# Transposing and pooling as one product, one engine to a bank's eviction, an early activation table, and a new order of the steps

## The chip, the cores and the metric

The kernel runs on one core of a Trainium2 chip. The core has five engines with queues of their own: TensorE (PE; its weight loads are shown as PEld), VectorE (DVE), ScalarE (ACT), GpSimd (POOL) and SyncE (SP), which issues most of the transfers. Each takes its instructions in the order in which they were written and waits at semaphores. The metric is the device time of one execution in microseconds, the median over several runs. 1.2 and 2.4 GHz are the two levels of TensorE's clock; the profile gives the granted clock as a share of the upper one.

## The reference

Two parts follow each other. First attention over `q`, `k`, `v` of shape (2, 8, 576, 64), batch, heads, tokens and channels, as the sum of two kinds:

```python
q_d, k_d, v_d = means of q, k, v over groups of 4 tokens      # 144 groups
out_d   = softmax(q_d k_d^T / 8) v_d                          # pooled attention
out_up  = repeat(out_d, 4, axis=2)
mask    = abs(pos[:, None] - pos[None, :]) < 4                # a band of 7 tokens
out_loc = softmax(where(mask, q k^T / 8, -1e9)) v             # local attention
x = (out_up + out_loc).transpose(0, 2, 1, 3).reshape(1152, 512)
```

Then a mixture of four experts over all 1152 tokens, each with weights 512 x 1024 and 1024 x 512:

```python
p = domain_probs / (domain_probs.sum(-1, keepdims=True) + 1e-9)
out = sum over e of p[:, e:e+1] * (maximum(x @ w1[e], 0) @ w2[e])
```

All inputs and the output are 32-bit floats.

## The kernel before

**Attention.** There are four attention blocks, a0 to a3: two batches, and of each the two halves of 288 tokens. A half is three tiles (t = 0, 1, 2) of 96 tokens. A tile of `q` or `k` is loaded with tokens on the partitions, 96 x 512, and has to stand with channels on the partitions. The step `k00t.0` (batch 0, half 0, tile 0) or `a0.qt.0` does this on TensorE: four transposes of 96 columns into one PSUM bank (line 391). For batch 0's keys and for a0's queries, nine tiles in all, four more products with a 96 x 24 pooling matrix (line 397) put the sums over four tokens beside them in the same bank. Two eviction steps follow, `k00te.0` for the tokens and `k00tp.0` for the sums; the table `ENGINE` gives each of them to ScalarE (A), VectorE (V) or GpSimd (G). The banks of these steps come from a pool of three (`ps_g`), so that a fourth tile waits for the first one's eviction.

Local scores are the steps `a0.sc0.0` and so on: 64 small products per tile (line 561) with, in a0 alone, a product of the identity with the mask ahead of them (line 551). `max`, `sub`, `exp`, `sum`, `rec`, `norm` are the softmax, `blk` transposes of 32 x 32 on VectorE, and `pv` the product with `v`. The pooled attention has the steps `ds` (scores, line 721), `dm`, `de`, `da`, `db`, `dq` (softmax), `dt` (transposes), `dc`, `dv` and `xd`. `v01s` and `v00s` are the pooled `v` of batch 0 (line 479). `xs`, `xh` and `xl` add both kinds up and split the result into a high and a low part; every large product is taken as three products of such parts.

**Experts.** Expert 0 runs in four chunks of tokens, m00 to m03: `m` is the first product (line 828), `r` and `l` evict it, `o` is the second (line 853). Chunk m00 needs only a0's result, m01 also a1's, m02 part of a2's, and m03 all of a3's, so the chunks lie between the steps of attention. The weights are loaded raw (`raw100`), and split by `whi` and `wlo`. Experts 1 to 3 follow (the late experts, lines 1084 and 1273), from the step `p110` on.

**The order.** Every step is a small function with a name. The list `ORDER` names all of them, and each engine's queue is its steps in that order; nothing is scheduled at run time. `WARM` gives the products of zeros that the steps `warm0` to `warm4` run on TensorE, in units of half a 512-column product. The helpers' lines 178, 180, 184 and 186 record most evictions of both engines. SP's loads stand in the same list, and a load whose target is still being read waits on SP with all loads behind it.

Of the kernel before, what the change touches and what calls it, by code (L numbers as in the profile page):

```python
# [21 lines left out]
ORDER = """
    k01r.0 a0q.2 pool warm0 k01t.0 a0.qt.2 k00r.1 k00t.1 k01r.1 kstart0 k00tp.1 k01r.2 k01tp.0 a0.start k01te.0 warm1
    k01t.1 k00te.1 k01te.1 a0q.0 k01tp.1 a0.qtp.2 a0.qte.2 k01t.2 a0.qt.0 a0q.1 k00r.0 mask a0.qt.1 a0.qtp.1 k01te.2
    a0.qte.0 a0.qtp.0 clear0 k00r.2 k01tp.2 v01n.1 clear1 k00t.0 a0.qte.1 vw00e vw00 k00t.2 k00tp.2 k00tp.0 warm2
    a0.ds0 k00te.2 k00te.0 a0.sc0.0 a0.dm0 a0.de0 a0.ds1 a0.dm1 a1q.2 a0.sc0.1 a0.de1 a0.max0 a0.da0 warm3 a0.ds2
    a0.db0 a0.dq0 a0.sub0 a0.da1 a0.db1 a0.sc1.0 a0.dt0 a0.sc1.1 a0.exp0 a0.sum0 a0.dc0 a0.dm2 a0.ds3 a0.dm3 v01n.0
    a0.sc2.0 a0.max1 a0.dq1 a0.dt1 a0.dc1 a1q.0 a0.de2 a0.da2 a0.sc2.1 a1.qt.2 a0.max2 a0.de3 a0.sub2 a0.exp2 poolw
    a1.start a1.qte.2 a0.sub1 a0.da3 a0.exp1 a0.rec0 a0.sum2 a0.rec2 a0.norm0 a1.qt.0 a0.db2 a0.norm2 a0.blk0.1
    a1.qte.0 v01n.2 v01s v01de vw01 a0.dq2 a1q.1 a0.db3 a0.sum1 a1.qt.1 a1.qte.1 a0.rec1 a0.blk0.0 vw02 v00s a0.norm1  # L30
    a0.blk1.0 v00de a1.sc1.1 a1.sc1.0 a1.qd.1 a0.dq3 a0.dt3 a0.dc3 a0.dv0 a0.dv1 raw100 a0.pv0 whi100.0 wlo100.0
    whi100.1 wlo100.1 a1.qd.0 a0.blk1.1 a0.blk2.1 a0.dt2 a0.dc2 a0.blk2.0 a0.dv2 a1.sc2.1 a0.dv3 a2q.0 a0.xd a0.xs0
    a0.xh0 warm4 a1.ds0 a1.ds1 a1.dm1 a0.pv1 a1.dm0 a1.de1 a1.de0 a1.sc0.1 a0.xs1 a0.xh1 a0.xl1 a1.da1 a1.db1 a0.pv2
    a1.sc2.0 a0.xs2 k10r.1 a0.xh2 a0.xl2 a1.sc0.0 a2q.2 a1.ds2 a1.ds3 k11r.2 a1.dq1 a1.madd0 a0.xl0 raw101 whi101.1
    kstart1 a1.max0 a1.dt1 vw03 m00.m0 a1.dc1 k10r.2 a1.da0 wlo101.1 m00.r0 a1.db0 m00.m1 m00.m2 k10t.2 a1.madd1
    a1.dq0 whi101.0 a2.start a1.sub0 a1.dt0 raw200 a1.dm2 a1.max1 a1.dm3 a1.de2 wlo101.0 m00.m4 m00.l0 m00.r1 a1.madd2
    a1.max2 a1.sub2 m00.l1 m00.r2 a1.dc0 k10r.0 k10t.0 a1.de3 whi200.1 a1.exp0 a1.sum0 k10t.1 a1.da2 wlo200.1 a1.da3
    a1.sub1 k10te.2 k10te.0 a2q.1 a2.qt.1 a2.qte.1 m00.l2 whi200.0 wlo200.0 m00.m7 a1.rec0 praw k11r.1 k10te.1 k10d.0
    a1.db3 a1.dq3 k11t.1 k11r.0 k11te.1 k11t.0 k11te.0 raw201 a1.norm0 a1.blk0.0 a2.qt.2 m00.r7 a1.exp2 a1.sum2 m00.m3
    m00.r3 m00.l7 a1.exp1 a1.dv0 a1.blk0.1 m00.r4 a1.sum1 vw04 a1.db2 a2.qt.0 a1.rec1 m00.l4 v10n.0 a2.qte.0 k11t.2  # L40
    a2.qte.2 a1.dq2 m00.m5 a1.rec2 k11te.2 a1.dv1 vw05e a1.norm2 a1.dt3 whi201.0 a2.qd.0 k11d.1 a1.dt2 m00.r5 a1.norm1
    m00.l5 m00.o10 a1.dc2 a2.qd.1 a1.dv2 a1.pv0 a1.blk2.1 m00.l3 v10n.1 a1.dc3 a1.dv3 a1.xd a1.xs0 v10d.0 a1.blk2.0
    a2.sc1.1 m00.o00 m00.m6 m00.r6 a3q.0 k11d.0 a2.ds0 a3q.1 a1.blk1.1 a2.dm0 a2.sc2.0 wlo201.0 a1.blk1.0 a2.sc2.1
    a2.sc0.0 a2.sc0.1 a2.madd0 vw10e a2.de0 a2.da0 a2.db0 a2.sc1.0 a2.madd1 vw05 a1.pv2 a1.xh0 a2.max0 a2.sub0
    a3.start a1.pv1 a1.xs2 a1.xh2 vw11 m00.l6 a1.xs1 m00.o01 a2.madd2 a2.max1 a2.sub1 whi201.1 a2.ds1 a2.dm1 a2.de1
    a2.dq0 a1.xl0 wlo201.1 a2.da1 a2.exp0 a2.sum0 a3q.2 m00.o11 m00.o12 a2.db1 m00.o13 a2.exp1 a1.xh1 m00.o02 m00.o03
    a2.max2 a2.sub2 v11n.1 a2.exp2 a3.qt.1 a2.sum2 a2.rec2 a2.dt0 v10d.1 a3.qt.2 a1.xl2 a3.qte.2 a1.xl1 m01.m6 gate
    a3.qte.1 k10d.1 a2.ds2 m01.r6 v11n.0 v11d.0 m00.g0 m01.l6 a2.rec0 a2.ds3 a2.dm3 a2.de3 a2.da3 a2.db3 m01.m3 m01.r3
    vw14 a2.sum1 m01.l3 a2.rec1 m01.m7 a2.dc0 m01.m1 m01.r1 v11d.1 a3.qt.0 a3.qte.0 a2.norm0 a2.dq1 a2.dt1 m00.g1
    a2.norm1 a2.blk1.1 a2.norm2 a2.dc1 a3.sc1.0 a2.blk1.0 a3.sc1.1 m01.l1 m01.r7 m01.l7 a3.sc2.1 a3.sc2.0 vw10 a2.dv0  # L50
    a2.dm2 a2.de2 a2.dv1 a2.blk0.1 a2.dq3 a2.dt3 a2.dc3 m01.m0 m01.r0 m01.m2 a2.blk0.0 a2.pv0 a2.da2 a2.db2 a2.dq2
    a3.qd.0 m01.r2 a3.madd2 a2.dt2 a2.dc2 a2.dv2 a2.dv3 vw15e a2.xd a2.xs0 a2.xh0 a2.blk2.1 m01.m5 a3.ds0 a2.blk2.0
    a2.pv1 m01.r5 m01.l2 a3.dm0 a3.de0 a3.sc0.0 a3.sc0.1 a3.madd0 m01.l0 m01.m4 a3.max0 m01.r4 m01.o00 m01.o01
    a3.madd1 m01.l5 a2.xs1 m01.l4 m01.o02 m01.o03 a3.qd.1 a3.max2 a3.sub2 a3.ds1 a3.dm1 a3.de1 a3.max1 a2.xh1 a2.xl0
    a3.sub1 m01.o10 a3.sub0 m01.o11 m01.o12 a3.da1 a3.db1 a2.xl1 vw12 a3.ds2 a3.dm2 a3.exp2 a3.exp1 a3.dq1 a3.sum1
    a3.dt1 m01.g0 a3.rec1 a3.de2 a3.da2 a3.db2 a3.dq2 a3.sum2 m01.o13 m02.m5 m02.r5 m02.l5 a3.dc1 a3.da0 a3.db0 m02.m4
    a3.exp0 a3.sum0 a3.dv1 a3.dt2 a3.dc2 a2.pv2 m01.g1 a3.rec0 m02.m3 m02.m1 a2.xs2 m02.r4 m02.l4 m02.r3 m02.l3
    a3.norm0 vw13 a3.blk0.0 a3.ds3 a3.dm3 a3.de3 a3.rec2 m02.r1 m02.m0 m02.r0 m02.m6 m02.m2 m02.r2 m02.r6 a3.dv2
    m02.l1 a3.blk0.1 a3.da3 a3.db3 a3.dq3 a3.dt3 a3.dc3 m02.l0 a2.xh2 a2.xl2 a3.norm2 a3.dq0 a3.pv0 m02.l2 a3.blk2.1
    a3.norm1 a3.blk1.0 a3.blk1.1 a3.dt0 a3.dc0 a3.dv0 a3.blk2.0 vw15 a3.dv3 a3.xd m02.m7 m02.r7 m02.o10 m02.l6 a3.xs0  # L60
    m02.o11 a3.xh0 a3.xl0 m02.o12 a3.pv2 a3.xs2 a3.pv1 m02.o00 m02.o01 m02.o02 a3.xs1 a3.xh2 m02.l7 m02.o13 a3.xh1
# [1372 lines left out]
```

## Time and profile before

| what | us |
|---|---|
| median of 3 runs | 461.78 (461.69 to 464.54) |
| the profiled execution | 460.38 |
| its span, first to last instruction | 458.5 |
| TensorE busy in the span | 444.9 |
| VectorE busy | 321.2 |
| ScalarE busy | 196.4 |
| GpSimd busy | 102.3 |

The busy time of an engine is the union of its instructions' times. A busy TensorE may still run at the lower clock, so its share is read beside the granted clock. The chain of waits follows the work that ended last back to the start: a piece of it is either work on an engine or time to issue.

### The profile page before, as it was taken

To read this page: it belongs to the slowest core of one execution; us is meant where nothing else is said; L and a number is where in the kernel's file an instruction comes from. 1 tells how busy PE (TensorE), PEld (TensorE's weight loads), DVE (VectorE), ACT (ScalarE), POOL (GpSimd) and SP (SyncE) were. 2 spreads that over 40 slices of the span, in tenths; PEclk is the share of its full clock that TensorE was granted. 3 is DMA by queue.
4 is the path that set the end of the run, shared out by engine and by line. 5 is a ranking of instruction groups with operands and counts; after the bars stand their busy time and mean duration, and the time that the engine had idled before them with its cause. 6 is when DMAs were issued, how large, how long until landed. Compare 5 with 4: busy or idle time off the path is not lost.

```text
span 458.5 us, 10026 instructions
## 1 busy us (share of the span) xinstructions
PE 444.9 (97%) x4181; PEld 420.4 (92%) x4181; DVE 321.2 (70%) x569; ACT 196.4 (43%) x389; POOL 102.3 (22%) x142
## 2 busy tenths in 40 slices
...
PEclk8578999999999999999999999999999999999999
...
GB/s 171 116 183 113 181 226 42 121 4 24 4 44 46 2 1 43 183 143 76 76 126 93 70 207 93 47 75 91 112 93 114 164 91 48 46 52 91 44 92 162
DMA packets 75494, 42.52 MB, mean 93 GB/s; under 512 B 36920, under 2 KB 73400, under 8 KB 75448
## 3 DMA queue, kind: packets, MB, share of 16 engines
...
q14 instruction: 13, 0.11, 0.1%
...
## 4 chain that ended last, share of the span: by engine, by line
PE 95%; DVE 2%; ACT 1%; issue 1%; POOL 1%; DVEq 0%; ACTq 0%
PE ps L1084 29%; PE ps L1273 26%; PE ps L1286 4%; PE m03h L828 4%; PE m03o L853 4%; PE m01h L828 3%; PE m02h L828 3%; PE m00h L828 3%; PE m00o L853 2%; PE m02o L853 2%; PE m01o L853 2%; PE vs L479 1%; PE a_qt L391 1%; PE wps L274 1%; PE k00t L397 1%; PE k01t L397 1%
## 5 line engine op out<-in xcount | busy, mean ns | idle before, releaser
L1273 PE MATMUL ps<-slot,unit 128*128 128x256 f32 x1008 | 119.9, 280 | 1.1 <-DVE unit L1193 1.1
L1273 PEld LDWEIGHTS ps<-slot,unit 128*128 128x128 f32 x1008 | 119.0, 189 | 1.3 <-DVE unit L1193 1.3
L1084 PE MATMUL ps<-xhi,slot 128*128 128x288 f32 x384 | 66.4, 294 | 0.0
L1084 PE MATMUL ps<-xc,slot 128*128 128x288 f32 x432 | 60.4, 295 | 0.0
L1084 PEld LDWEIGHTS ps<-xc,slot 128*128 128x128 f32 x432 | 58.3, 188 | 0.1
L1084 PEld LDWEIGHTS ps<-xhi,slot 128*128 128x128 f32 x384 | 56.3, 188 | 0.1
L1133 POOL DMA_DIRECT2D raw<-in_moe_w_dram x15 | 19.5, 1297 | 143.1 <-DVE slot L1139 82.6
L1096 ACT ACTIVATE H<-ps 128x288 f32<-128x288 f32 x72 | 27.6, 412 | 50.8 <-PE ps L1084 50.8
L184 ACT CAST slot<-raw 128x1024 fp32r<-128x1024 f32 (+1 forms) x33 | 41.7, 1280 | 9.1 <-DVE raw L1032 9.1
L1100 DVE TENSOR_TENSOR H<-H,ps 128x288 f32<-128x288 f32 x72 | 29.7, 449 | 20.6 <-PE ps L1084 20.5
L1038 DVE TENSOR_TENSOR slot<-raw,slot 128x1792 fp32r<-128x1792 f32 x12 | 24.3, 2022 | 25.3 <-PE ps L1084 21.1
L1084 PE MATMUL ps<-xlo,slot 128*128 128x288 f32 x192 | 41.1, 295 | 0.0
L1188 ACT ACTIVATE unit<-H 128x1024 fp32r<-128x1024 f32 x18 | 19.1, 1062 | 28.9 <-PE ps L1273 17.4
L1084 PEld LDWEIGHTS ps<-xlo,slot 128*128 128x128 f32 x192 | 30.7, 188 | 0.0
L1171 DVE SCALAR_TENSOR_TENSOR H<-H 128x1024 f32<-128x1024 f32 (+1 forms) x18 | 28.1, 1575 | 3.5 <-ACT H L1098 3.2
L1184 ACT ACTIVATE unit<-H 128x512 fp32r<-128x512 f32 (+1 forms) x24 | 20.0, 844 | 23.2 <-DVE H L1100 13.6
L1139 DVE TENSOR_TENSOR slot<-raw,slot 128x1024 fp32r<-128x1024 f32 x21 | 25.3, 1218 | 2.4 <-ACT slot L184 2.4
L1197 DVE SCALAR_TENSOR_TENSOR unit<-H,unit 128x1024 fp32r<-128x1024 f32 x18 | 22.0, 1222 | 7.1 <-ACT unit L1188 7.0
L1193 DVE SCALAR_TENSOR_TENSOR unit<-H,unit 128x512 fp32r<-128x512 f32 (+1 forms) x24 | 22.5, 952 | 1.5 <-ACT unit L1184 1.5
L1295 DVE SCALAR_TENSOR_TENSOR acc<-ps,npr,acc 128x256 f32<-128x256 f32 x48 | 20.7, 477 | 3.1 <-PE ps L1273 2.9
L636 DVE STREAM_TRANSPOSE ptb<-pmb 32x256 f32<-32x256 f32 x48 | 20.9, 435 | 2.1 <-PE a0pv L645 0.7
...
## 6 DMA issues: line engine op xcount, KB each, us to landing
...
```

The lines of the kernel that those rows point to most:

```text
L184: nc.scalar.copy(out_, in_)
L828: nc.tensor.matmul(ps[:, :n], w[:, d, cc:cc + P], x[:, d, n0:n0 + n], start=i == 0, stop=i == len(terms) - 1,)
L853: nc.tensor.matmul(ps[:, cs], T[f"{nm}t{f}"][:, hpart, cc:cc + P], w[:, f % 4, cs], start=f == 0 and x == 0, stop=f == KF - 1 and x == 2,)
L1038: engine(f"wo{e}{i}").tensor_tensor(w1tile(i, 1), raw1(e, i), f32(w1tile(i, 0)), ALU.subtract)
L1084: nc.tensor.matmul(bank(acc_, n, i)[:, :NH // 2], w[:, d * P:(d + 1) * P], x[:, d, n * (NH // 2):(n + 1) * (NH // 2)], start=u == 0 and fi ...
L1096: nc.scalar.mul(dst, at, -1.0)
L1100: nc.vector.tensor_tensor(dst, dst, at, ALU.add)
L1139: engine(f"bo{e}{m}").tensor_tensor(w2tile(m, 1), raw2(q), f32(w2tile(m, 0)), ALU.subtract)
L1171: nc.vector.scalar_tensor_tensor(at[o], at[x], 0.0, at[y], ALU.max, op)
L1193: nc.vector.scalar_tensor_tensor(o, x, 0.0, y, ALU.max, ALU.subtract)
L1197: nc.vector.scalar_tensor_tensor(o, x, -1.0, y, ALU.mult, ALU.subtract)
L1273: nc.tensor.matmul(ps[:, t * 256:t * 256 + 256], a[:, f, t * P:t * P + P], b[:, f], start=first_ and (t, f, x) == (0, 0, 0), stop=(t, f, x ...
```

## The change

- The tile `ident` becomes `idt`, whose first 24 columns are a pooling matrix and whose next 128 are the identity. For the nine tiles that are pooled on TensorE, one ordinary product of 120 columns takes the place of a transpose of 96 and a product of 24. The other fifteen tiles keep their transposes.
- One step evicts both parts of a bank, on one engine; the steps `tp` are gone.
- The pooling matrices are made by a memset and two selections instead of copies and additions. The values that `v01s` needs get a step of their own, `poolm`.
- A copy of one column on ScalarE at the very start brings the activation table load there.
- `WARM` goes from 16, 2, 2, 4, 2 to 24, 2, 2, 2; `ENGINE` and `ORDER` are new for everything up to `endfirst`; from `p110` on the order is as before.

```diff
-WARM = [16, 2, 2, 4, 2]
+WARM = [24, 2, 2, 2]
 ORDER = """
-    k01r.0 a0q.2 pool warm0 k01t.0 a0.qt.2 k00r.1 k00t.1 k01r.1 kstart0 k00tp.1 k01r.2 k01tp.0 a0.start k01te.0 warm1
...
+    clear0 mask k00r.0 clear1 pool warm0 k00t.0 kstart0 k00te.0 a0q.0 k00r.1 a0.start a0.qt.0 k00t.1 k01r.1 k01t.1
+    a0q.1 a0.qte.0 vw00e a0.qt.1 a0.qte.1 k00te.1 a0.sc0.0 a0.sc0.1 a0.max0 a0.sub0 k01r.2 k01t.2 k01te.2 a0q.2
...
-    ident = big.tile([P, P], F32, name="ident")
+    idt = big.tile([P, TT // R + P], F32, name="idt")
+    ident = idt[:, TT // R:]
...
+    nc.scalar.copy(prs[:, 0:1], wz[:, 0:1])
...
+    def averaging(dst, pattern, base):
+        nc.gpsimd.memset(dst, 1.0)
+        for sign, b0 in ((-1, -base), (1, base + R - 1)):
+            nc.gpsimd.affine_select(
+                out=dst, in_=dst, pattern=[[sign * st, n] for st, n in pattern], compare_op=ALU.is_ge, fill=0.0,
+                base=b0, channel_multiplier=-sign,
             )
...
+    step("pool", "G", [], lambda: averaging(idt[:, :n_pool], [[R, n_pool]], 0))
+    step("poolm", "G", ["pool"], pooling_values)
     step("poolw", "G", [], pooling_windows)
...
+        n = TT // R if pooled_to is not None else 0
+        w = TT + n
+
         def pe(t):
             pt = g_tile(f"{nm}.{t}")
             for hp in range(HP):
-                nc.tensor.transpose(
-                    pt[:, hp * TT:(hp + 1) * TT], T[src][:, t, hp * P:(hp + 1) * P], ident[:TT, :TT]
-                )
-            if pooled_to is not None:
-                g0, n = HP * TT, TT // R
-                for hp in range(HP):
-                    nc.tensor.matmul(
-                        pt[:, g0 + hp * n:g0 + (hp + 1) * n], T[src][:, t, hp * P:(hp + 1) * P], pool_m[:TT, 2 * n:3 * n],
-                        start=True, stop=True,
-                    )
+                o, x = pt[:, hp * w:(hp + 1) * w], T[src][:, t, hp * P:(hp + 1) * P]
+                if n:
+                    nc.tensor.matmul(o, x, idt[:TT, :w], start=True, stop=True)
+                else:
+                    nc.tensor.transpose(o, x, ident[:TT, :TT])
...
+        def evict(t):
+            pt = T[f"{nm}.{t}"][:, :HP * w].rearrange("p (h c) -> p h c", h=HP)
+            ev(f"{nm}e.{t}", dst(t), pt[:, :, n:])
+            if n:
+                ev(f"{nm}e.{t}", pooled_to(t), pt[:, :, :n])
```

TensorE's queue at the head of the program, before (`k01t`, `k00t` and `a_qt` are tiles of keys and of queries in PSUM, `acc` holds the loaded rows, `early` the pooling matrix, `wps` the warming):

```order
L274 MATMUL wps<-wz 128x512 x8
L391 MATMUL k01t_137<-ident,acc 128x96 x4
L397 MATMUL k01t_137<-early,acc 128x24 x4
L391 MATMUL a_qt_146<-ident,acc 128x96 x4
L397 MATMUL a_qt_146<-early,acc 128x24 x4
L391 MATMUL k00t_156<-ident,acc 128x96 x4
L397 MATMUL k00t_156<-early,acc 128x24 x4
L274 MATMUL wps<-wz 128x512
L391 MATMUL k01t_177<-ident,acc 128x96 x4
L397 MATMUL k01t_177<-early,acc 128x24 x4
```

and in the changed kernel, up to the ninth tile and the second tile's scores (`a0sl` and `a0sb` are a0's local scores):

```order
L270 MATMUL wps<-wz 128x512 x12
L392 MATMUL k00t_147<-idt,acc 128x120 x4
L392 MATMUL a_qt_162<-idt,acc 128x120 x4
L392 MATMUL k00t_167<-idt,acc 128x120 x4
L392 MATMUL k01t_173<-idt,acc 128x120 x4
L392 MATMUL a_qt_184<-idt,acc 128x120 x4
L542 MATMUL a0sl<-mask,idt 128x128 x2
L552 MATMUL a0sl<-kT_152,a0qT 24x32 x32
L392 MATMUL k01t_234<-idt,acc 128x120 x4
L392 MATMUL a_qt_256<-idt,acc 128x120 x4
L392 MATMUL k00t_261<-idt,acc 128x120 x4
L392 MATMUL k01t_268<-idt,acc 128x120 x4
```

A tile is one row instead of two, and the local scores of a0's first tile have moved ahead of the last four tiles; before, they stood behind all nine and behind the first pooled scores.

ScalarE's queue at the head, before:

```order
L184 ACT_TABLE_LOAD
L184 COPY kT_166<-k01t_137 128x4x96
L184 COPY kT_166<-k00t_156 128x4x96
L178 ACTIVATE a0qd<-a_qt_146 128x4x24
L184 COPY kT_166<-k01t_193 128x4x96
L178 ACTIVATE a0qT<-a_qt_202 128x4x96
```

and in the changed kernel:

```order
L194 ACT_TABLE_LOAD
L194 COPY prs<-wz 128x1
L178 ACTIVATE a0qT<-a_qt_162 128x4x96
L178 ACTIVATE a0qd<-a_qt_162 128x4x24
L178 ACTIVATE a0qT<-a_qt_184 128x4x96
L178 ACTIVATE a0qd<-a_qt_184 128x4x24
```

The table load now belongs to a copy that needs no tile, and the two parts of a tile stand one behind the other.

GpSimd's queue around the first weights of expert 0 (`raw`, `whi`, `wlo`; `a0pd` and `pmb` are softmax tiles), before:

```order
L632 TENSOR_TENSOR pmb_101<-pmb_101,a0sr_518 128x8x32
L766 TENSOR_TENSOR a0pd_447<-a0pd_447,a0dsr 72x288
L357 TENSOR_TENSOR wlo_600<-raw_587,whi_598 128x256 x8
L672 TENSOR_TENSOR xlo<-a0x_696,xhi 128x4x96
L672 TENSOR_TENSOR xlo<-a0x_651,xhi 128x4x96
```

and in the changed kernel:

```order
L757 TENSOR_TENSOR a0pd_474<-a0pd_474,a0dsr 72x288
L757 TENSOR_TENSOR a0pd_429<-a0pd_429,a0dsr 72x288
L353 TENSOR_TENSOR wlo_612<-raw_511,whi_600 128x256 x4
L663 TENSOR_TENSOR xlo<-a0x_614,xhi 128x4x96
L353 TENSOR_TENSOR wlo_715<-raw_664,whi_668 128x256 x4
```

Four of the eight pieces of the first low weights have left GpSimd (they are one instruction of 1024 columns on VectorE now), and one of its two low parts of a0.

## Rows read from the trace of the kernel before

**Rows 1.** The page, forty slices of the span: granted clock of TensorE in tenths.

```profile
PEclk8578999999999999999999999999999999999999
```

**Rows 2.** Stages: us; busy us (count) of PE, PEld, DVE, ACT, POOL; clock; DMA; GB/s.

```profile
0.00:4.65 4.65, 3.59 (x9) 2.71 (x10) 0.24 (x6) 0.00 (x0) 3.60 (x19) 1.00 0.66 129
4.65:8.06 3.41, 3.41 (x36) 3.41 (x34) 0.00 (x0) 0.00 (x0) 1.32 (x2) 1.00 1.37 204
8.06:28.54 20.48, 18.71 (x153) 17.17 (x152) 4.94 (x18) 5.39 (x17) 0.00 (x0) 0.50 0.86 163
28.54:35.37 6.83, 5.22 (x175) 3.87 (x162) 3.97 (x17) 2.54 (x12) 4.43 (x19) 1.00 0.69 113
35.37:38.78 3.41, 3.41 (x9) 1.38 (x8) 3.13 (x16) 1.48 (x4) 1.43 (x4) 0.50 0.60 169
38.78:53.00 14.22, 12.81 (x315) 8.48 (x314) 11.00 (x26) 7.92 (x21) 9.64 (x16) 1.00 0.47 145
53.00:184.60 131.60, 128.09 (x1351) 114.19 (x1350) 98.41 (x213) 45.85 (x122) 36.67 (x48) 1.00 0.25 56
184.60:458.50 273.90, 269.64 (x2160) 269.17 (x2159) 199.49 (x277) 133.27 (x215) 45.24 (x37) 1.00 0.50 99
```

**Rows 3.** Chain of waits to 25 us: start us, us, engine, tile, line, count.

```profile
1.06 3.75 PE wps L274 x8
...
5.14 0.83 PE k01t L397 x8
5.98 0.37 PE a_qt L391 x4
...
9.10 1.28 ACT L184
...
13.42 0.71 PE k01t L391 x4
14.12 1.59 PE k01t L397 x8
```

**Rows 4.** Chain of waits from 25 us on.

```profile
26.75 1.15 PE a0sl L551 x4
27.90 0.78 PE a0sl L561 x64
...
29.34 0.65 PE a0sd L721 x8
...
31.54 0.64 PE a0sl L551 x4
32.19 0.27 PE a0sl L561 x29
...
33.09 1.61 issue
...
34.93 1.05 PE a_qt L391 x8
35.98 4.03 PE vs L479 x6
...
53.02 4.36 PE m00h L828 x36
...
78.75 8.43 PE m00o L853 x36
```

**Rows 5.** Timeline of TensorE in two short windows at 30 us: start, us, instructions.

```profile
29.92 0.49 PE L551 MATMUL a0sb<-mask,ident 128*128 128x128 f32 x2
...
29.92 0.71 PE L551 MATMUL a0sb<-mask,ident 128*128 128x128 f32 x4
```

**Rows 6.** Timeline of GpSimd and ScalarE up to 12 us.

```profile
3.66 1.84 POOL L261 MEMSET ptb<- 128x1024 f32 x2
...
10.39 0.48 ACT L184 COPY kT<-k01t 128x384 f32<-128x384 f32 x1
```

**Rows 7.** One stage, from the first part of a0's result to a1's.

```profile
52.50:87.90 35.40, 34.33 (x489) 30.89 (x489) 31.63 (x82) 17.62 (x52) 22.78 (x31) 1.00 0.67 144
```

More of the change, by code (lines that the diff above doesn't have):

```diff
@@ L27 @@
[L27 to L51, printed above, removed]
@@ new lines @@
+    a0.blk0.0 a0.sc1.0 a0.sc1.1 a0.blk0.1 k01te.0 a0.ds0 a0.ds1 a0.dm1 a0.sc2.0 poolw a0.dm0 a0.max1 a0.de1 a0.da1
+    a0.db1 a0.sc2.1 a1.start a1q.1 a1.qt.1 a1q.2 warm1 a1.qt.2 a0.de0 a0.sub1 a1.qte.2 a1.qte.1 a0.da0 v01n.2 vw00
+    a0.dq1 a0.max2 a0.sub2 warm2 a0.dt1 a0.ds2 a0.db0 a0.dm2 a0.dc1 a1q.0 a0.exp2 a0.exp1 a0.sum1 a0.de2 a0.ds3 poolm
+    v01s a0.dq0 a0.dt0 v01de a0.rec1 a0.dm3 a0.norm1 a0.sum2 a0.rec2 a0.norm2 a1.sc1.1 a0.blk1.1 a0.de3 a0.da2 a0.dc0
+    vw01 a0.blk1.0 a0.pv0 a0.da3 a1.qt.0 a1.qte.0 a0.db2 a0.db3 vw02 a0.dq3 raw100 a0.blk2.0 v00s a1.qd.0 a1.sc2.1
@@ new lines @@
+    a1.sc2.0 v00de a0.dv0 a0.dt3 a0.dv1 a0.blk2.1 a0.dq2 a0.dc3 warm3 a0.dt2 a0.dc2 a0.dv2 a0.dv3 a0.pv1 a0.xd
+    whi100.0 whi100.1 a0.pv2 wlo100.1 a0.xs0 a0.xs1 a0.xs2 a0.xh0 a1.sc1.0 a1.sc0.0 a0.xh1 a0.xl1 a0.xh2 a0.xl2 a1.ds0
+    a1.dm0 raw101 praw whi101.1 a1.ds1 a1.dm1 a1.madd2 k11r.1 wlo100.0 a0.xl0 m00.m1 a1.max2 a1.de0 a1.da0 a1.db0
+    a1.de1 a1.dq0 m00.m0 a1.madd1 wlo101.1 a1.max1 a1.sub1 whi101.0 wlo101.0 m00.m3 a1.qd.1 m00.r1 m00.r0 m00.l0
+    m00.m2 vw05e k10r.0 a2q.2 m00.r3 a1.da1 a1.db1 a1.dq1 raw200 whi200.0 a1.sub2 m00.r2 a1.dt0 a1.dc0 a1.dv0 a1.sc0.1
@@ new lines @@
+    m00.l3 k11r.2 a2q.0 a1.ds2 a1.dm2 a2q.1 a1.de2 a1.exp2 a1.ds3 a1.dt1 m00.l1 a1.madd0 a1.max0 m00.m6 vw03 a1.exp1
+    m00.r6 a1.dm3 m00.m4 a1.de3 a1.da2 a1.sub0 a1.exp0 m00.l6 a1.dc1 a2.qt.2 a2.start a2.qte.2 kstart1 k10t.0 k10te.0
+    k11t.2 k10r.2 a2.qt.1 a2.qte.1 k11te.2 wlo200.0 k10r.1 a2.qt.0 m00.m5 vw04 a2.qte.0 k11r.0 a1.sum2 a1.rec2 v10n.0
+    a1.sum0 a1.rec0 a1.db2 k10t.2 a1.norm0 k10te.2 a1.da3 a1.dq2 a1.db3 a1.sum1 k11t.1 k11te.1 k10t.1 gate k10te.1
+    a1.rec1 a1.norm1 a1.dv1 a1.dq3 a1.dt3 a1.dc3 vw05 a1.blk0.1 a1.dt2 m00.l2 a1.dc2 a1.blk1.0 a1.blk0.0 a3q.1
@@ new lines @@
+    a1.norm2 a2.sc1.0 a2.sc0.1 m00.r5 a1.blk1.1 a1.dv2 a1.dv3 m00.l5 a1.xd a1.pv0 a1.xs0 a1.xh0 a1.xl0 whi200.1 a1.pv1
+    k11t.0 a1.xs1 a1.xh1 m00.m7 m00.o10 a1.blk2.1 m00.r7 a1.blk2.0 a1.pv2 k11te.0 k11d.0 a2.sc2.1 m00.l7 a2.sc0.0
+    a2.sc1.1 a1.xs2 a1.xh2 a2.sc2.0 a2.madd0 a2.max0 m00.r4 a2.qd.0 m00.o00 a1.xl1 wlo200.1 m00.o11 m00.l4 k10d.0
+    a2.ds0 raw201 whi201.0 a1.xl2 a3q.0 m00.o01 a2.ds1 a2.sub0 a2.exp0 whi201.1 wlo201.1 m01.m1 a2.sum0 a2.madd1
+    a2.max1 wlo201.0 m00.o12 m00.o02 m01.r1 m00.o03 a2.dm1 a2.de1 a2.da1 a2.db1 a2.dq1 a2.rec0 k10d.1 v11n.1 m01.l1
@@ new lines @@
+    a2.qd.1 m01.m3 a2.dm0 a3.qt.1 a2.dt1 a3q.2 a3.start a2.sub1 a2.de0 a2.da0 a2.madd2 v10d.0 m01.r3 m00.g0 a3.qt.2
+    k11d.1 v11n.0 m01.m5 a2.exp1 a2.sum1 a2.rec1 a2.max2 a2.sub2 a3.qte.1 m01.l3 a3.qte.2 a2.norm1 a2.ds2 a2.ds3
+    a2.norm0 m00.o13 a2.exp2 a2.dc1 a2.db0 a2.dm3 m01.r5 m01.l5 a2.blk0.1 a2.blk1.1 m01.m0 m01.m4 a3.qt.0 a2.de3
+    a2.da3 a2.db3 a2.dq3 v10n.1 a2.sum2 a2.rec2 a2.dq0 a2.dt0 m01.r4 v10d.1 a2.dm2 a2.de2 m00.g1 a2.norm2 a3.sc2.0
+    a2.blk0.0 m01.r0 m01.l0 vw11 a2.da2 a2.db2 a3.sc2.1 a3.qte.0 a3.sc1.0 a3.qd.0 m01.m7 v11d.1 a2.dq2 a3.qd.1 m01.m6
@@ new lines @@
+    m01.g0 a3.ds3 a3.dm3 a3.dt2 m01.g1 a3.exp2 a3.de3 vw15 a3.da3 a2.xl1 m02.m0 m02.r0 a2.xs2 a2.xh2 m02.l0 a3.da0
+    a3.db3 a3.db0 a3.norm1 m02.m7 a3.sum0 a3.rec0 a3.blk1.1 vw13 vw14 a3.norm0 a3.blk1.0 m02.r7 a3.dc2 m02.m3
+    a3.blk0.0 m02.r3 a3.dq0 a3.dq3 m02.m1 m02.r1 m02.l1 a2.xl2 a3.dv1 a3.dv2 a3.dt3 a3.dt0 a3.dc3 m02.l3 a3.sum2
+    m02.m2 m02.r2 m02.l2 a3.dc0 a3.blk0.1 m02.m4 m02.m6 m02.r4 m02.l4 a3.pv0 a3.rec2 a3.norm2 m02.r6 m02.l6 a3.dv0
+    a3.dv3 m02.m5 a3.blk2.0 a3.blk2.1 a3.xd a3.pv1 a3.xs1 a3.xh1 m02.r5 a3.xs0 a3.xh0 a3.pv2 a3.xs2 m02.l5 a3.xh2
@@ L222, with pooling_values @@
     )
-    def pooling():
-        z = 2 * (TT // R)
-        nc.gpsimd.memset(pool_m, 0.0)
-        nc.gpsimd.tensor_copy(
-            pool_m[:TT, z:z + TT // R].rearrange("p (g o) -> p g o", o=1),
-            ident[:TT, :TT].rearrange("p (g r) -> p g r", r=R)[:, :, 0:1],
-        )
-        for r in range(1, R):
-            nc.gpsimd.tensor_tensor(
-                pool_m[:TT, z:z + TT // R].rearrange("p (g o) -> p g o", o=1),
-                pool_m[:TT, z:z + TT // R].rearrange("p (g o) -> p g o", o=1),
-                ident[:TT, :TT].rearrange("p (g r) -> p g r", r=R)[:, :, r:r + 1], ALU.add,
-            )
+    def averaging(dst, pattern, base):
[4 more added lines that the diff above has]
+                base=b0, channel_multiplier=-sign,
+            )
+    n_pool = TT // R
+    def pooling_values():
+        nc.gpsimd.memset(pool_m, 0.0)
+        nc.gpsimd.tensor_copy(pool_m[:, 2 * n_pool:3 * n_pool], idt[:, :n_pool])
     def pooling_windows():
-        z = 2 * (TT // R)
-        gb = QB // R
         nc.gpsimd.memset(pool_w, 0.0)
-        for j in range(4):
-            for r in range(R):
-                o = pool_w[32 * j:32 * j + 32, z + gb * j:z + gb * j + gb].rearrange("p (g o) -> p g o", o=1)
-                d = ident[32 * j:32 * j + 32, 32 * j + R:32 * j + R + QB].rearrange("p (g r) -> p g r", r=R)[:, :, r:r + 1]
-                nc.gpsimd.tensor_tensor(o, o, d, ALU.add)
-    step("pool", "G", [], pooling)
+        averaging(pool_w[:, 2 * n_pool:3 * n_pool].rearrange("p (j g) -> p j g", j=4), [[32, 4], [R, QB // R]], R)
+    step("pool", "G", [], lambda: averaging(idt[:, :n_pool], [[R, n_pool]], 0))
+    step("poolm", "G", ["pool"], pooling_values)
     step("poolw", "G", [], pooling_windows)
@@ L482, in vkeep @@
                     copy(f"v{b}{half}de", vd_tile()[:, half], T[f"vs{b}{half}"][:G].rearrange("p (h d) -> p h d", h=H))
-                need = [f"vw{b}{t}" for t in range(NT)] + ["poolw"] if half == 0 else [f"v01n.{t}" for t in range(NT)] + ["pool"]
+                need = [f"vw{b}{t}" for t in range(NT)] + ["poolw"] if half == 0 else [f"v01n.{t}" for t in range(NT)] + ["poolm"]
                 step(f"v{b}{half}s", "P", need, vsums)
```

114 lines of the change are left out of this document (49 added, 65 removed).

## The prediction

> **What bounds the kernel now.** I read the strip of forty slices first [rows 1]: the granted clock of TensorE is below 9 tenths only in the first four. The table of stages comes second [rows 2]. From 184.6 us on nothing but the late experts runs (TensorE busy 269.64 of 273.9 us at full clock), and from 53.0 to 184.6 us it is busy 128.09 of 131.6 us. So both later stages are TensorE's, and 3.5 us is all the idle time of the middle one. The first 53 us are different: from 8.06 to 28.54 us the granted clock is 0.50 (1.2 GHz) while TensorE is busy 18.71 of 20.48 us, and again 0.50 from 35.37 to 38.78 us. The chain of waits says what it did there [rows 3]: tile after tile of transposing (L391) and pooling (L397), back to back. At 5.14 us, at full clock, eight pooling instructions of 24 columns take 0.83 us and four transposes 0.37 us; at 13.42 and 14.12 us, at half clock, 0.71 and 1.59 us. So the kernel loses time at the head in two ways: a slow clock and a second set of small products. The last a0 scores end at 34.93 us, and the first product of expert 0 starts at 53.02 us [rows 4]. I read the changed order on each engine only for which work stands where.
>
> **The change part by part.** *One product of 120 columns.* It removes 36 transposes and keeps 72 instructions (four products of a tile are eight instructions, each with its own weight load). Its price is not in the trace. The nearest row is the mask product of 128 columns at full clock: two instructions 0.49 us, four 0.71 us, so 0.11 us for each further one [rows 5]. Below it stands the 24-column row, 0.83/8 = 0.104 us; above it 0.64/4 = 0.16 us, a group of four with its lead-in [rows 4]. I take 0.11, since 120 columns are nearest to 128 and the instructions follow each other: 0.88 us a tile at full clock (0.83 to 1.28) against 1.20 before at full clock and 2.30 at half.
>
> 24 columns and 128 cost nearly the same here, so the transposing rides along [rows 3, 5]. The Trainium skill (Perfetto Trace Analysis, Transposes) says the contrary as a rule: a logical transpose should be a transpose and not a standard matmul. By that rule the 96 columns would be paid on top of the pooling's; the rival "columns add up" below prices this from rows. I take the rows' side, because the pooling product is there in either case.
>
> *Clock.* Mask products of 128 columns ran from 26.75 us on, and the clock was full from 28.54 us [rows 2, 4]; it fell at 35.37 us, after 1.61 us of waiting among products of 32 and 72 columns, and came back at 38.78 us, during 512-column products of v (4.03 us) [rows 2, 4]. Products of 120 columns, back to back, are nearer to the mask products than to those of 24, so I take full clock from the start on.
>
> *Warming.* Twelve products instead of eight. The eight take 3.75 us [rows 3], 0.47 each; m00o's of the same width take 8.43/36 = 0.23 at full clock [rows 4]. The clock record starts at 4.65 us with full clock, so four more end at about 5.6 us (6.7 at half).
>
> *Pooling matrix.* GpSimd now clears ptb first (1.84 us [rows 6]) and builds the matrix by a memset and two selections after it. Before, memset, copy and three additions stood there; clearing ended at 5.50 us. The new matrix stands at about 5 us, hidden behind the warming; without that cover it would cost what lies beyond 4.6 us, half a microsecond.
>
> *Table and eviction.* The activation table load (1.28 us at 9.10, a link of the chain [rows 3]) goes ahead of all data, and this wait goes. An eviction was split over two engines, each with its own wait; now one engine does both parts, 0.48 us for the tokens [rows 6] and for the pooled quarter an estimated 0.25 or less. Two engines take turns, so 0.73 us a tile each lies beside two products of 0.88, with three banks between.
>
> *Loads.* 0.60 MB have moved by 4.65 us (129 GB/s), then 204 GB/s [rows 2]; a tile of 0.197 MB (96 x 512 x 4 bytes) comes every 0.96 us, the ninth by 10.4 us. TensorE starts the ninth after 14 us, so SP's queue does not hold it. SP then stands until a0's third q tile has been read, which comes earlier too. All that expert 0 needs before its first product (some 19 tiles' worth of q, k, v and one megabyte of weights, 4.8 MB) takes 23.5 us at 204 GB/s, under the 35 below.
>
> *Order.* Local scores of a0 now start after five tiles, so VectorE's softmax begins among the tiles. Head up to the last a0 scores: 5.6 + 9 x 0.88 + 3 x (0.64 + 2 x 0.27) + 0.65 (one pair of pooled scores) = 17.7; with 0.5 for evictions 18.2 us, against 34.93. From there to the first m00 product it was 53.02 - 34.93 = 18.1 us, a chain through softmax, values and the splitting of weights on all engines. The new stretch holds one pair of pooled scores more from a0 and one less from a1; 3.41 us of it were at half clock (1.7 to win), and GpSimd's eight pieces of the first weights become four, with one VectorE instruction for the rest. I take 17.0 (15 to 21): m00 starts at 35.2 us. The middle stage is TensorE's 131.6 plus what moved into it, a pair of pooled scores and half a local one (0.65 + 0.3), plus 1.5 for waits that a new order of a1 to a3 brings (0 to 8): 134.1. The late experts stand in the same order: 273.9.
>
> Sum: 35.2 + 134.1 + 273.9 = 443.2 us against the span of 458.5, so 15.3 less. The profiled execution took 460.38 us and would take 445.1; the median of the runs is 1.4 higher, 461.78, so I predict **446.5 us**. With the bounds of price, stretch and waits the forecast's own range is 442 to 452.
>
> **The rivals.** *The clock stays at half in the head.* The trace of before has transposes and 24-column products always mixed, so it cannot tell which of them kept the clock down; 96 of 120 columns are still a transposing. Then: start 6.7, nine tiles at 1.76, three scores at 1.15 + 0.78 [rows 4], pooled scores 1.3 (twice 0.65), together 29.6 instead of 17.7; some of it is won back once the scores run, as at 28.54. 453 to 458, say 456. Chance 0.12. The Trainium skill (TensorE: Matmul & The Clock Gate, Part 4) says that transpose mode does not count as busy for the clock. By that the change, which takes transpose mode away, raises the clock; the half clock of rows 2 agrees, but no run here separates it.
>
> *VectorE becomes the bound in a1 and a2.* From 52.5 to 87.9 us it is busy 31.63 of 35.4 us [rows 7], and the new order starts this stretch 18 us earlier with the same work. For it: TensorE executes in order, and a value product waits for two transposes of VectorE; if these come late, everything behind stands. Against it: VectorE did only 4.94 us in the 20.48 us of half clock [rows 2], so it has room to work ahead. Price 4 to 10 us of new TensorE waits, 453.5. Chance 0.12.
>
> *Columns add up*: a tile costs its 96 and its 24 columns separately, 0.88 + 0.83. Nine times 0.83 is 7.5: 454. Rows 5 speak against it. Chance 0.03.
>
> *Loads hold it after all*: the weights come late behind SP's wait, the first m00 product starts at some 46 us. 457, within 1%. Chance 0.04.
>
> *Slower*: one mechanism, TensorE held at the value products of a1, a2 and a3 by VectorE. Three such holds of 6.7 us each eat the 15.3 us and 4.6 more; it decides when TensorE's idle time of the middle stage goes from 3.5 to over 24 us: 467. The 3.5 us are the sum over all its waits [rows 2], so 0.03.
>
> **How the numbers follow.** The forecast has 0.66. 446.5 is its time. 441 to 455 takes it in with most of the VectorE case and half of the clock case; about 0.8. What can be told from no change is 1%, 4.6 us, so faster means below 457.2: the forecast, VectorE, columns and most of the clock case, 0.89. Within 1%: loads and the rest of the clock case, 0.08. Slower 0.03.
>
> **What would show it.** In the changed kernel's table of stages the clock should be 1.00 from about 5 us to some 20 us. A tile's eight instructions should span about 0.9 us; the last a0 scores should end near 18 us, the first m00 product start near 35 us, and the first product of the late experts near 169 us, with 5 us or less of TensorE idle between them. The late stage should be 274 us again. A granted clock of 0.50 over the tiles, spans of 1.3 us or more, or VectorE named before TensorE's waits from 40 to 80 us would make it wrong; so would a first m00 product past 42 us.

## The result and the profile after

The changed kernel takes **443.25 us** (median of 4 runs, 442.67 to 445.04) against 461.74 for the kernel before; the ratio is 0.9593, 95% interval 0.9547 to 0.9639. That is 18.5 us less. I had predicted 446.5, 15.3 less, in a range of 441 to 455: the side and the range hold, and the gain came out 3.2 us larger than forecast. The profiled execution took 442.67 us with a span of 440.9, 17.6 less than the span of before. Over all sessions of this document the kernel before lies between 457.05 and 466.18 us and the changed one between 442.19 and 445.04; the ratios leave out the slow executions at its upper end.

The clock strip of the page answers to [rows 1]: the four low slices at its left end are gone.

```profile
PEclk9999999999999999999999999999999999999999
```

The stages, with the columns of [rows 2] (expert 0 and the late experts are cut at their first product in the timeline, which in the kernel before stands at 52.82 and 184.42 us, 0.18 ahead of the cuts in [rows 2]): to the rise of the clock, to the end of a0's scores, to the first product of expert 0 (m00), to the late experts, to the end.

```profile
0.00:6.29 6.29, 5.16 (x12) 4.10 (x13) 3.37 (x12) 1.48 (x2) 4.31 (x18) 1.00 0.73 149
6.29:18.88 12.59, 12.59 (x286) 11.81 (x285) 7.21 (x22) 4.15 (x15) 1.34 (x5) 1.00 1.01 171
18.88:36.06 17.18, 16.08 (x305) 10.10 (x299) 14.23 (x40) 9.42 (x29) 9.46 (x14) 1.00 0.88 217
36.06:165.16 129.10, 128.44 (x1393) 114.30 (x1393) 99.50 (x215) 49.41 (x132) 42.13 (x58) 1.00 0.30 65
165.16:440.90 275.74, 271.53 (x2161) 271.06 (x2159) 199.40 (x277) 133.43 (x215) 45.24 (x37) 1.00 0.49 99
```

The clock of 1.00 in the first row is no reading: the record of the clock begins with its rise at 6.29 us. The twelve warming products ahead of it take 0.43 us each, against 0.23 for products of that width at full clock [rows 4].

Three numbers carry the result. From 6.29 to 18.88 us TensorE is busy for all 12.59 us at full clock; before, the stretch of half clock alone took 20.48. Expert 0 starts at 36.06 us instead of 52.82. And in the middle stage TensorE is idle for 0.66 us (129.10 less 128.44) instead of 3.51. The late stage is 1.7 us *longer* than before (275.74 against 274.08 at the same cut); point 6 below says what is known of it.

The chain of waits from the start (start us, us, engine, tile, line, count), against [rows 3]:

```profile
1.13 5.39 PE wps L270 x12
6.52 0.89 PE k00t L392 x8
7.41 0.89 PE a_qt L392 x8
8.30 0.89 PE k00t L392 x8
...
10.98 0.45 PE a0sl L542 x4
11.44 0.67 PE a0sl L552 x48
...
22.60 6.54 DMA raw<-in_moe_w_dram
```

A tile is one line of 0.89 us; [rows 3] shows 1.20 for one at full clock and 2.30 at half. Up to 14 us no eviction and no table load is a link any more. From there on the chain runs through SP's queue to the load of the first weights, which lands at 29.14 us. That was my rival on loads. But TensorE has its own work beside it and is idle for only 1.1 us from 6.29 to 36.06, so this chain costs no more than that.

### The profile page after: what moved, and what is told of

The parts are those of the page before. It is cut to its first block, busy times and chain, and to the rows that moved or that the text cites. A ratio compares the mean times of both kernels' runs of the same rounds, so it can differ in the third digit from the quotient of the medians.

```text
span 440.9 us, 9961 instructions
## 1 busy us (share of the span) xinstructions
PE 433.8 (98%) x4147; PEld 411.4 (93%) x4147; DVE 323.7 (73%) x564; ACT 197.9 (45%) x390; POOL 102.5 (23%) x132
## 4 chain that ended last, share of the span: by engine, by line
PE 90%; DVE 4%; SPq 2%; DMA 1%; ACT 1%; issue 1%; POOL 0%; DVEq 0%; ACTq 0%
PE ps L1075 30%; PE ps L1264 27%; PE ps L1277 4%; PE m03h L819 4%; PE m03o L844 4%; PE m00o L844 3%; PE m01h L819 3%; PE m02o L844 3%; PE m01o L844 2%; PE m00h L819 2%; DMA raw<-in_moe_w_dram 1%; SPq L323 1%; PE m02h L819 1%; PE wps L270 1%; PE a_qt L392 1%
## 5 line engine op out<-in xcount | busy, mean ns | idle before, releaser
L1264 PE MATMUL ps<-slot,unit 128*128 128x256 f32 x1008 | 121.3, 282 | 1.1 <-DVE unit L1184 1.1
L1264 PEld LDWEIGHTS ps<-slot,unit 128*128 128x128 f32 x1008 | 120.4, 189 | 1.3 <-DVE unit L1184 1.3
```

The costliest lines, as they stand in the source:

```text
L1264: nc.tensor.matmul(ps[:, t * 256:t * 256 + 256], a[:, f, t * P:t * P + P], b[:, f], start=first_ and (t, f, x) == (0, 0, 0), stop=(t, f, x ...
```

## Experiments

Twelve runs were made, each timed against the kernel before in its own session (medians of 460 to 461.5). Between sessions the ratios are the safer comparison. "m00" and "late" are the starts of the first product of expert 0 and of the late experts in the profiled execution.

| kernel | median us | ratio to before (95%) | m00 | late |
|---|---|---|---|---|
| changed kernel | 443.25 | 0.959 (0.955 to 0.964) | 36.1 | 165.2 |
| two_products | 456.31 | 0.989 (0.982 to 0.996) | 47.4 | 179.0 |
| plain96_24 | 466.15 | 1.011 (1.007 to 1.014) | 55.8 | 187.8 |
| transp_120 | 448.67 | 0.971 (0.966 to 0.977) | 38.9 | 171.5 |
| old_order_one | 452.44 | 0.979 (0.972 to 0.985) | 42.5 | 172.2 |
| old_order_again (the same) | 452.68 | 0.985 (0.979 to 0.991) | 45.0 | 174.6 |
| old_order_table | 448.09 | 0.976 (0.969 to 0.984) | 38.2 | 169.6 |
| old_order_swap | 446.25 | 0.971 (0.965 to 0.977) | 38.9 | 168.8 |
| after_again (changed kernel) | 443.00 | 0.966 (0.962 to 0.970) | 36.2 | 165.4 |
| no_table | 443.25 | 0.967 (0.962 to 0.972) | 36.8 | 166.4 |
| split_evict | 444.96 | 0.972 (0.967 to 0.977) | 38.3 | 167.8 |
| warm16 | 442.56 | 0.966 (0.960 to 0.971) | 35.7 | 165.2 |
| warm_first_only | 441.83 | 0.961 (0.955 to 0.966) | 35.1 | 164.8 |

**What keeps the clock down: transposes, or products of 24 columns?** Three kernels change only the nine pooled tiles of the changed kernel.

two_products:

```diff
-                    nc.tensor.matmul(o, x, idt[:TT, :w], start=True, stop=True)
+                    nc.tensor.transpose(o[:, n:], x, ident[:TT, :TT])      # all four, then
+                    nc.tensor.matmul(o[:, :n], x, idt[:TT, :n], start=True, stop=True)
```

> The changed kernel, but each of the nine pooled tiles is again four transposes and then four products of 24 columns; order, evictions, table load and warming stay new. Theory (the product of 120 columns keeps the clock up): granted clock 0.50 over the tiles, a tile 2.30 us instead of 0.89, nine tiles 12.7 us more, some of it won back where the new order lets TensorE wait less; late experts start near 175 us instead of 165.2, time about 453 us. Rival (the new order and the longer warming keep the clock up): clock 1.00, a tile 1.20, nine tiles 2.8 us more, time about 446 us.

plain96_24, no transposes:

```diff
-                    nc.tensor.matmul(o, x, idt[:TT, :w], start=True, stop=True)
+                    nc.tensor.matmul(o[:, n:], x, ident[:TT, :TT], start=True, stop=True)
+                    nc.tensor.matmul(o[:, :n], x, idt[:TT, :n], start=True, stop=True)
```

> The changed kernel, but each of the nine pooled tiles is four ordinary products of 96 columns with the identity and then four of 24 columns: no transposes, but the small products. Theory A (the transposes keep the clock down): clock 1.00 over the tiles, a tile 0.88 + 0.83 = 1.7 us, nine tiles 7.5 us more than now, time about 450 us. Theory B (the products of 24 columns keep it down): clock 0.50, a tile 3.2 to 3.4 us, nine tiles over 20 us more, time about 462 us.

transp_120, no products of 24 columns:

```diff
+                    nc.tensor.transpose(o[:, n:], x, ident[:TT, :TT])      # all four, then
                     nc.tensor.matmul(o, x, idt[:TT, :w], start=True, stop=True)
```

> The changed kernel, but each of the nine pooled tiles has four transposes of 96 columns ahead of the product of 120 columns, which writes over them: double work, no products of 24 columns. Theory A (the transposes keep the clock down): clock 0.50 over the tiles, a tile 0.71 + 1.78 = 2.5 us, nine tiles 14.4 us more, time about 456 us. Theory B (the products of 24 columns keep it down): clock 1.00, a tile 0.37 + 0.89 = 1.26 us, nine tiles 3.3 us more, time about 446.5 us.

The stages of two_products (columns as in [rows 2]), cut where the granted clock changed:

```profile
5.07:11.89 6.82, 6.82 (x65) 6.60 (x64) 1.84 (x7) 0.63 (x2) 0.19 (x1) 1.00 1.35 204
11.89:28.96 17.07, 17.07 (x266) 15.67 (x266) 6.71 (x23) 4.35 (x17) 2.27 (x9) 0.50 0.63 103
```

of plain96_24:

```profile
12.22:39.52 27.30, 27.30 (x311) 25.84 (x310) 7.30 (x26) 4.34 (x17) 2.44 (x9) 0.50 0.43 106
```

and of transp_120, from the rise of the clock to the first product of expert 0, on to the late experts, and a part of the latter stretch:

```profile
5.15:38.90 33.75, 32.38 (x623) 25.52 (x622) 21.79 (x64) 13.56 (x42) 10.89 (x20) 1.00 0.92 191
38.90:171.53 132.63, 130.09 (x1393) 115.41 (x1393) 99.46 (x215) 49.38 (x132) 42.12 (x58) 0.99 0.29 61
66.59:70.00 3.41, 3.41 (x9) 2.31 (x7) 3.38 (x7) 1.35 (x2) 1.75 (x3) 0.50 0.02 5
```

In the first two TensorE is busy without a gap, 17.07 of 17.07 and 27.30 of 27.30 us, and yet at 0.50. In the third, all 36 transposes are there and the clock stays at 1.00 over the tiles and the scores. The other executions agree: the mean clock of the whole span was 0.974 to 0.977 in the four runs of two_products, 0.963 to 0.974 in the ten of plain96_24, 0.996 to 1.000 in the four of transp_120 and 0.995 to 1.000 in ten of the changed kernel. So it was not the transposes. That is theory B: in this order the tiles with products of 24 columns fell to half clock, and those with products of 120 in their place did not, with transposes or without. The new order alone does not help two_products. Two limits: tiles of 96 columns alone were not run, and old_order_again below ran at half clock without a product of 24 columns.

Undoing the one product costs 13.1 us (456.31 against 443.25; I had expected about 10). plain96_24 came out 4.2 us over theory B's 462 and transp_120 2.2 over its 446.5. In the middle stage of transp_120 TensorE is idle for 2.5 us, and the 3.41 us from 66.59 us on are at half clock. Two of its four runs had a clock of 1.000 and were 0.9 us faster.

The timeline of TensorE in plain96_24 and in transp_120 gives the prices at full clock (start us, us, instructions; the length includes the drain of the last one, so starts are compared):

```profile
5.95 1.03 PE L393 MATMUL k00t<-idt,acc 96*128 96x96 f32 x8
6.82 1.00 PE L398 MATMUL k00t<-idt,acc 96*128 96x24 f32 x8
7.66 1.11 PE L393 MATMUL a_qt<-idt,acc 96*128 96x96 f32 x8
```

```profile
5.84 0.49 PE L392 MATMUL k00t<-idt,acc 96*128 96x96 f32 x4
6.17 1.08 PE L395 MATMUL k00t<-idt,acc 96*128 96x120 f32 x8
7.09 0.49 PE L392 MATMUL a_qt<-idt,acc 96*128 96x96 f32 x4
```

Eight instructions of 96 columns take 0.87 us, of 24 columns 0.84, of 120 columns 0.92 with their lead-in; four transposes 0.33. The price is nearly that of the instruction, not of the columns, so 96 columns added to a product that is there anyway come almost for nothing.

**How much is the product in the old order?** old_order_one is the kernel before with line 391 and 397 made one product of 120 columns (and its matrix put beside the identity); ORDER, ENGINE, WARM and the split evictions are unchanged.

> The kernel before with its own order, engines, warming and split evictions; only the nine pooled tiles become one product of 120 columns. Theory (the clock is the larger part): clock 1.00 from 5 to 30 us, the last a0 scores end near 24 us instead of 34.9, the first product of expert 0 starts near 43 us, time about 451 us. Rival (the order is the larger part): TensorE waits for the evictions and loads of the old order instead, 36 transposes less are worth 3.3 us at full clock and 6.4 at half, time 455 to 458 us.

> The kernel before with its own order and only the product of 120 columns put in, unaltered, as the measure for the two kernels beside it. Both theories: 452 us, with TensorE waiting 2.1 us at 8.6 to 10.7 us for the fourth tile's bank.

By the ratios it gains 2.2 and 1.5%, 7 to 10 us. The last a0 scores end at 24.1 us in old_order_one, as forecast, and 452.44 us stand against the 451 of the theory: the clock is the larger part. Then the kernel stands at a wait. TensorE's timeline, and ScalarE's, of old_order_one (in brackets the idle time ahead, and what ended it):

```profile
10.70 2.04 PE L392 MATMUL k01t<-idt,acc 96*128 96x120 f32 x16 [2.13 <-ACT kT L185]
```

```profile
8.88 1.28 ACT L185 ACT_TABLE_LOAD   x1 [8.88 <-DVE kd L187]
10.17 0.48 ACT L185 COPY kT<-k01t 128x384 f32<-128x384 f32 x1
```

The fourth tile waits 2.1 us for the first tile's bank, which ScalarE empties late: the table load starts when VectorE's pooled eviction of that bank ends. In old_order_again the wait was the same and the clock fell behind it: at 12.07 us to 0.50, until 25.72, though TensorE then had work without a gap (two tiles a line in the timeline behind the stages).

```profile
5.24:12.07 6.83, 4.70 (x40) 4.31 (x38) 1.17 (x5) 2.30 (x4) 0.86 (x2) 1.00 1.36 204
12.07:25.72 13.65, 13.65 (x122) 11.44 (x122) 5.98 (x24) 3.69 (x14) 1.57 (x4) 0.50 1.09 212
```

```profile
12.15 3.74 PE L392 MATMUL a_qt<-idt,acc 96*128 96x120 f32 x16
15.68 3.62 PE L392 MATMUL k00t<-idt,acc 96*128 96x120 f32 x16
```

Here four tiles in a row, products of 120 columns alone, took 1.6 to 1.8 us each and the clock stayed at half. In the changed kernel these products ran on at a full clock; in this execution they did not bring it back. The eight runs of this kernel had mean clocks of 0.980 to 0.995, and mostly the lower the clock, the longer the run (449.78 us at 0.995, 454.11 at 0.981).

**Table load and evictions, one at a time.** old_order_table adds the early copy to old_order_one:

```diff
     nc.vector.memset(wz, 0.0)
+    nc.scalar.copy(prs[:, 0:1], wz[:, 0:1])
```

> The old order with one product, and the early copy of one column on ScalarE added. Theory (in the old order the table load stands behind a wait of ScalarE for VectorE, so it is a link of the chain): the load moves from 8.9 to 0.8 us, ScalarE's first eviction of a tile ends 1.3 us earlier, TensorE's wait of 2.1 us for the fourth tile's bank shrinks to 0.8, time about 1.3 us under the same kernel without it. Rival (loads or VectorE hold the head anyway): the wait goes elsewhere, time the same within 0.3 us.

old_order_swap instead lets ScalarE read the first bank first:

```diff
-... k00tp.1 k01r.2 k01tp.0 a0.start k01te.0 warm1
+... k00tp.1 k01r.2 k01te.0 a0.start k01tp.0 warm1
```

> The old order with one product, without the early copy, but the two evictions of the first tile change places: ScalarE's tokens first, VectorE's pooled sums behind. Theory (the table load is late only because the instruction behind it has a second wait, on VectorE, which stands ahead of the load): with one wait left the load runs at 0.8 us without any copy, ScalarE's first eviction starts near 6.4 us instead of 10.2, TensorE's wait of 2.1 us is gone, time 1.5 to 2.5 us under the same kernel unswapped. Rival (the load always comes when the first real work does): the load runs at 6.4 us, time 0.5 to 1.5 us under.

no_table takes the copy out of the changed kernel:

```diff
-    nc.scalar.copy(prs[:, 0:1], wz[:, 0:1])
```

> The changed kernel without the copy of one column at the start, so that the activation table load stands ahead of the first eviction on ScalarE. Theory (the new order hides most of it): the table load runs at 8.3 to 9.6 us, the first query bank comes free near 10.3 us instead of 9.0, and the fifth tile, which takes that bank at 10.1 us, waits 0.3 us; time 0 to 0.5 us over the changed kernel. Rival (it costs its whole length, as a link of the chain of the kernel before): a wait of TensorE of 1.3 us on ScalarE, time 1.3 us over.

ScalarE at the head of old_order_swap, and of no_table:

```profile
0.74 1.28 ACT L185 ACT_TABLE_LOAD   x1 [0.74 <-PEq L1416]
6.40 0.48 ACT L185 COPY kT<-k01t 128x384 f32<-128x384 f32 x1 [4.38 <-PE k01t L392]
```

```profile
0.81 1.28 ACT L178 ACT_TABLE_LOAD   x1 [0.81 <-PEq L1411]
8.83 0.49 ACT L178 ACTIVATE a0qT<-a_qt 128x384 f32<-128x384 f32 x1 [6.74 <-PE a_qt L391]
```

Neither has the early copy, and the load stands at 0.7 and 0.8 us. In the written order of the kernel before, the load has a wait of its own, and the chain of waits of its trace has that wait as a piece ahead of the load (ACTq is ScalarE's sequencer):

```
L184 ACT_TABLE_LOAD [waits DVE_49]
L184 COPY kT_166<-k01t_137 128x4x96 [waits PE_49]
```

```profile
9.05 0.02 ACTq L184
9.06 0.03 issue
9.10 1.28 ACT L184
```

The first eviction has two waits there, one for TensorE and one for VectorE's read of the same bank; the second one stands ahead of the load and holds it too. In old_order_swap and no_table, where one wait is left, the load went at once. So in the new order the copy does nothing (443.25 against 443.00; my theory there, 0 to 0.5 us, held, though for another reason: I expected the load at 8.3 us). In the old order both edits gave more than I had expected: 4.6 us for the copy instead of 1.3, and 6.4 for the swap instead of 1.5 to 2.5. The waits shrank, from 2.1 to 0.8 (as expected) and to 0.3 us. The rest goes with the clock, which in both profiles stayed full over all tiles and scores: its mean was 0.992 to 0.996 and 0.995 to 1.000 in their runs, 0.981 to 0.988 in those of old_order_again.

**One engine or two for a bank.** split_evict lets the other engine read the pooled quarter:

```diff
-                ev(f"{nm}e.{t}", pooled_to(t), pt[:, :, :n])
+                other = "V" if steps[f"{nm}e.{t}"][0] == "A" else "A"
...
+                    nc.scalar.copy(pooled_to(t), pt[:, :, :n])      # or nc.vector
```

> The changed kernel unaltered, on the same chip as the three kernels beside it, so that differences below 1 us can be read. Both theories: 443 us.

> The changed kernel, but of each pooled tile the tokens leave the bank on the same engine as now and the sums over four tokens on the other one of VectorE and ScalarE. Theory (which engine evicts is hidden by three banks): no wait of TensorE over the tiles, time within 0.5 us of the changed kernel. Rival (the second reader of a bank waits for the first, and what stands behind it on its engine with it, as at 8.4 to 10.4 us in the kernel before): TensorE waits 1 to 3 us among the tiles, time 1 to 3 us over.

Waits of TensorE in split_evict (engine, line, what it waited for: us, times, longest):

```profile
PE a0sd L721 <- DVE kd L409: 1.6, 1, 1.6
...
PE a0sl L561 <- DVE kT L186: 0.7, 1, 0.7
```

The rival is right: 2.0 us over (444.38 to 449.02 against 442.19 to 443.62), with two waits of together 2.3 us that the changed kernel doesn't have. It wasn't the banks that ran out; scores waited for keys whose eviction stood behind another engine's.

**Warming.** warm16 has `WARM = [16, 2, 2, 2]`, warm_first_only `[16, 0, 0, 0]`.

> The changed kernel with eight warming products ahead of the first tile instead of twelve. Theory (the last four only delay the tiles, and products of 120 columns bring the clock up as well): the first tile starts at 4.65 us instead of 6.4, at half clock at first, the clock is full from about 5 to 6.5 us on and stays so, time 0.8 to 1.7 us under the changed kernel unless the loads hold the tiles. Rival (the longer warming is what gets and keeps the clock up): granted clock 0.50 over several tiles, 0.9 us more for each, time 2 to 6 us over.

> The changed kernel with eight warming products ahead of the first tile and none later (the three single ones at 19.2, 19.8 and 30.4 us go too). Theory (TensorE's own work is the bound of the head, so each instruction taken out of it counts): the head is shorter by three times 0.27 us and by up to 0.5 us for the first four, time 1 to 1.3 us under the changed kernel, 442 us. Rival (the three keep the clock up among the small products of the softmax): granted clock 0.50 for a stretch between 19 and 36 us, 1.7 us more for each 3.4 us of it, time 1 to 4 us over.

In warm16 the first tile started at 4.7 us but ran at half clock, as did part of the second: 442.56 us (441.46 to 445.68), within the scatter of the changed kernel. So the clock rose without the last four warming products too, at 7.29 us during the second tile, and by the medians these four neither cost nor win anything. warm_first_only is the lowest median of all, 441.83 (441.10 to 443.39), 1.2 below after_again as its theory said; but the ranges overlap, the two ran on different chips, and the profiles put the late experts only 0.5 us earlier. A gain of 1 us is possible, not shown.

## Why the prediction was right, and where it was off

1. **The product.** 0.88 us a tile was forecast from the 128-column row; it is 0.89. The rule of the Trainium skill that spoke against it (Perfetto Trace Analysis, Transposes) is right for a tile that is only transposed, 0.33 against 0.87 us; it would have misled here, where the pooling product is issued anyway. "Columns add up" is out.

2. **The clock.** Full from 6.29 us on, as forecast. I had left open which instruction held it down; in these tiles half clock went with the products of 24 columns, not with the transposes. The page TensorE: Matmul & The Clock Gate of the Trainium skill, Part 4, has transposes not counting as busy. The trace neither needs nor refutes that: with all transposes in place the clock stayed full (transp_120), without any in the tiles it was half (plain96_24). My choice, full clock, was right, and the transposing as a suspect was wrong. That products of 120 columns always run at full clock is not so: old_order_again had four such tiles at half.

3. **Warming**: 5.6 us forecast, 6.5 measured. I priced four more products at 0.23 us because the clock record of before begins at 4.65 us with full clock. In the profiled execution it rises at 6.29 us, and all twelve took 0.43 us apart. But this is not a fixed cost of the kernel: in after_again the clock rose at 4.33 us and the first tile started at 5.47 us, where the execution above had 6.36.

4. **From a0's scores to expert 0**: 17.0 forecast, 17.18 measured; with the 0.9 from warming, m00 at 36.06 instead of 35.2. In after_again the parts are the other way round: the scores ended at 17.99 us, and the next stretch took 18.2, with the clock at 0.50 from 31.64 to 35.05 us. The same 32 products there and in the execution above:

```profile
31.63 2.76 PE L636 MATMUL a0pv<-ptb,vw 128*64 128x96 f32 x32
```

```profile
32.51 1.56 PE L636 MATMUL a0pv<-ptb,vw 128*64 128x96 f32 x32
```

That m00 comes at 36.06 and 36.22 us in the two is luck: two shifts of about 1 us cancel.

5. **The middle stage**, the step that was furthest off: 131.6 + 0.95 of work moved in + 1.5 for new waits = 134.1 us; measured 129.1. I took it that a new order brings waits and gave no chance to one that removes them. The idle time went from 3.51 to 0.66 us, and the busy time grew by 0.35 instead of 0.95. That is the order's work: the four profiles of the old order with one product have 2.9 to 3.1 us idle in this stage, the six of the new order with the changed kernel's tiles 0.7 to 1.4. But the stage is shorter than before's 131.60 by 2.5 us, and only 0.8 of these are the order's, since it also moved work in. In old_order_swap, with the old order, the stage takes 129.87 us:

```profile
38.91:168.78 129.87, 126.81 (x1352) 113.18 (x1350) 98.67 (x213) 45.98 (x122) 36.67 (x49) 1.00 0.27 58
```

6. **The late stage**: 273.9 forecast (274.08 at the cut used here), 275.74 measured, with the same instructions at full clock. It isn't the new order: old_order_one, which keeps the order of the kernel before, has the same 275.8.

```profile
172.22:448.00 275.78, 271.54 (x2161) 271.07 (x2159) 199.52 (x277) 133.42 (x215) 45.21 (x37) 1.00 0.49 98
```

All thirteen profiles of the later kernels have 275.7 to 275.8 here; the one execution that I predicted from is 0.6% shorter. Expert 0 differs the other way: the products with `whi` in m01 and m02 took 281 to 283 ns on average before and 279 in the changed kernel and in old_order_swap, which is part of the 1.7 us that the middle stage lost without the new order. All later kernels also share the wider tile `idt`. Whether that tile's place in memory does this, or the one execution of before was an odd one, is open.

The three errors, +0.9, -5.0 and +1.8, make the 2.3 us between the forecast span of 443.2 and the measured 440.9. The mechanism of the head was forecast rightly, the price of the tile and the clock; that of the middle stage was not. That the total lies closer than the middle stage is luck, because the errors partly cancel.

7. **Table and evictions.** "This wait goes" came true. The copy that I named would do it in the old order (old_order_table); in the new one it wasn't needed, because one engine per bank left the first eviction a single wait. And I gave the merged eviction 0.5 us of cost and no gain; undone, it costs 2.0 us.

Where the 18.5 us come from, in steps that were run: the product of 120 columns in the old order 7 to 10 us, the first bank's evictions and with them the table load 6.4 (452.68 to 446.25 in one session), everything else in the new order about 3 (446.25 to 443.25, in different sessions). The steps aren't additive: taken out of the finished kernel, the product is worth 13.1.
